# Layer 2's first product in two runs of 256 columns instead of one of 512

## The chip, the cores and the metric

The kernel runs on one core of a Trainium2 chip. The metric is the time on the device of one execution in microseconds; of several executions the median counts.

## What is computed

Attention with a local window and a few global keys over 2 batches of 8 heads, 768 positions and 64 columns per head, and behind it two feed-forward layers on 1536 rows of 512 columns:

```
def reference(**kwargs):
    attn_out = _attn_ref(**attn_kwargs)
    B, H, S, D = attn_out.shape
    x = np.ascontiguousarray(attn_out.transpose(0, 2, 1, 3)).reshape(B * S, H * D)
    x = _moe_ref(x=x, **moe_kwargs)
    return _moe2_ref(x=x, **moe2_kwargs)

def _moe_ref(x, w_in, w_out):        # w_in 512x2048, w_out 2048x512
    h = x @ w_in
    g = np.maximum(0.01 * h, h)
    return (g @ w_out).astype(np.float32)

def _moe2_ref(x, w_in, w_out, a, b):
    h = x @ w_in
    h2 = h * h
    h3 = h2 * h
    P = a[0] + a[1] * h + a[2] * h2 + a[3] * h3
    Q = 1.0 + np.abs(b[0]) * np.abs(h) + np.abs(b[1]) * h2
    g = P / (Q + 1e-06)
    return (g @ w_out).astype(np.float32)
```

The weights arrive as 64-bit floats and are decoded on the chip.

## The kernel before

Each number that goes into a large product is kept as a sum of two parts, a high one and a low one (xh and xl, gh and gl, and two halves of each weight tile), in a 4-byte format. A product of two such numbers is three matmuls: high by high, high by low, low by high.

**Attention** goes first, head pair by head pair. A score (line 377, tile sc) is a matmul of 64 partitions: the even head of a pair lies on partitions 0 to 63, the odd one on 64 to 127, and their matmuls are written alternately. The moving operand has 256 columns, or 128 for a head's first block. The values (lines 434 and 435, tile o) have 65 columns.

**The layers** are 96 units: two layers, in each 3 tiles of 512 rows of x, in each 16 blocks of 128 of the 2048 inner columns. In the code l is the layer, t the tile, f the block, and TT = 512. A unit's first product, `h_steps` (line 606, tile h), is 12 matmuls: 4 blocks c of the 512 inner rows by the three pairs of parts. The stationary operand is a 128x128 piece of the weight tile, the moving one 512 columns of xh or xl, and all 12 add into one bank of PSUM (512 numbers per partition) that `bank()` gives out in turn from two. Then the activation reads the whole bank: `act_1` in layer 1, `emit_act_2` in layer 2, on ScalarE, VectorE and GpSimd, and leaves gh and gl. The second product, `emit_y`, is again 12 matmuls of 512 columns: line 727 in layer 1, line 729 in layer 2, where a piece of gh or gl is stationary. Line 660 makes gl, in layer 2 mostly on GpSimd.

The order on each engine is that of the code. The loop in `run` writes for each unit u first h of u, then y of unit u - 2, and then the activation; so TensorE has h and y in turn. A weight tile of layer 2 comes back decoded from DRAM while layer 1 ends. Another path of the program, with attention over all keys, is skipped by a branch for these inputs; it holds a second copy of the layers that doesn't run.

Of the kernel before, what the change touches and what calls it, by code (L numbers as in the profile page):

```python
# [17 lines left out]
P = 128  # L18
# [7 lines left out]
def attention_moe_moe2(  # L26
# [15 lines left out]
    nc = tc.nc  # L42
# [7 lines left out]
    NK = DM // P  # L50
    NF = DFF // P
    TT = 512
# [62 lines left out]
    xh = xpool.tile([P, NK, NT], F32R, name="xh")  # L115
    xl = xpool.tile([P, NK, NT], F32R, name="xl")
# [465 lines left out]
    class Layers:  # L582
# [16 lines left out]
        def h_steps(self, u):  # L599
            l, t, f = self.units[u]  # L600
            wt = (self.w1, self.w2)[l][f]
            cs = slice(t * TT, (t + 1) * TT)
            h = self.state["h", u] = self.bank()
            for c in range(NK):
                for n, (m, xs) in enumerate(((0, xh), (0, xl), (1, xh))):
                    nc.tensor.matmul(  # L606
                        h,
                        wt[:, m, c * P : (c + 1) * P],
                        xs[:, c, cs],
                        start=c == 0 and n == 0,  # L610
                        stop=c == NK - 1 and n == 2,
                    )
                yield

        def new_g(self, u):
            gh, gl = (self.tpool.tile([P, TT], F32R, tag=n, name=n) for n in ("gh", "gl"))
# [448 lines left out]
```

## Time and profile before

| what | us |
|---|---|
| median of 3 runs | 642.52 |
| lowest and highest of them | 641.34, 643.16 |
| span of the profiled execution, first to last instruction | 639.8 |
| median less that span | 2.7 |
| TensorE busy | 625.5 |
| VectorE busy | 472.1 |
| ScalarE busy | 438.6 |
| GpSimd busy | 207.8 |

The profile gives for its execution only the span, not a time of its own with what lies around it; the last 2.7 us come from setting the span against the median. The recorded duration of a matmul holds its way through the array and overlaps with the next, so the rate of matmuls is read from their starts, or from blocks of the chain of waits.

### The profile page before, as it was taken

The page shows a single profiled execution, that of the slowest core. Times are in us where ns is not written, and L with a number is a line of the kernel's source. Part 1 is how long each engine was busy: PE and PEld are TensorE (multiplying, and loading weights), DVE is VectorE, ACT ScalarE, POOL GpSimd, SP SyncE. Part 2 cuts the span into 40 slices and gives each one's busy share as a digit, 9 for nine tenths or more (in the row PEclk, how much of TensorE's full clock was granted, in tenths as well). Part 3 has the DMA queues.
Part 4 walks back from the last instruction along what each step waited for, and adds up shares of the span by engine and source line. Part 5 has one row for each costly group of instructions (what it writes and reads, how often), then busy time and mean ns, then how long its engine had stood idle before and what let it go on. Part 6 is the DMA issues. An engine that isn't in the chain of part 4 may idle for free.

```text
span 639.8 us, 9604 instructions
## 1 busy us (share of the span) xinstructions
PE 625.5 (98%) x3264; PEld 526.1 (82%) x3264; DVE 472.1 (74%) x933; ACT 438.6 (69%) x830; POOL 207.8 (32%) x220
## 2 busy tenths in 40 slices
PE   6999999999999999999999999999999999999995
PEld 4999998888888888888888888888888888888884
DVE  6888988887886555555444479997777777897784
ACT  4788997777876545455334477876677888866672
POOL 2887884344443433332000002222222222112220
PEclk9999999999999999999999999999999999999999
DMA  8775861755268776765323310000023332100002
GB/s 189 171 190 139 184 155 67 252 192 191 73 202 241 216 234 209 225 220 171 95 97 98 100 33 34 1 1 0 1 92 106 96 97 72 48 19 1 2 0 73
DMA packets 81323, 73.35 MB, mean 115 GB/s; under 512 B 51248, under 2 KB 67888, under 8 KB 81264
## 3 DMA queue, kind: packets, MB, share of 16 engines
q1 hardware_dynamic: 80752, 72.11, 38.4%
q8 instruction: 28, 0.46, 0.3%
q0 software_dynamic: 80, 0.39, 0.1%
q14 instruction: 31, 0.25, 0.1%
q10 hardware_dynamic: 432, 0.13, 0.1%
HBM read 60.69 MB, written 11.93 MB: 113 GB/s over the span
## 4 chain that ended last, share of the span: by engine, by line
PE 95%; DVE 3%; DMA 1%; issue 0%; ACT 0%; SPq 0%; DVEq 0%
PE h L606 41%; PE y L729 21%; PE y L727 20%; PE pt L413 3%; PE sc L377 3%; PE o L435 2%; PE o L434 2%; PE h L306 2%; DVE sn L388 1%; PE h L199 1%; DMA qr<-in_q_dram 1%; PE o L432 0%; DVE pts L421 0%; DVE xl L205 0%; DVE w L164 0%
## 5 line engine op out<-in xcount | busy, mean ns | idle before, releaser
L606 PE MATMUL h<-xh,w 128*128 128x512 f32 x768 | 253.0, 390 | 0.0
L606 PEld LDWEIGHTS h<-xh,w 128*128 128x128 f32 x768 | 144.2, 188 | 30.0
L606 PE MATMUL h<-xl,w 128*128 128x512 f32 x384 | 149.4, 389 | 0.0
L660 POOL TENSOR_TENSOR gl<-u,gh 128x512 fp32r<-128x512 f32 x44 | 57.0, 1296 | 265.0 <-PE y L729 129.6
L727 PE MATMUL y<-gh,w 128*128 128x512 f32 x384 | 126.1, 389 | 0.0
L729 PE MATMUL y<-w,gh 128*128 128x512 f32 x384 | 125.6, 389 | 0.0
L155 POOL TENSOR_TENSOR dec<-dec,wraw 128x512 int32<-128x512 int32 x48 | 64.0, 1342 | 82.7 <-DVE wraw L142 79.0
L727 PEld LDWEIGHTS y<-gh,w 128*128 128x128 f32 x384 | 72.1, 188 | 15.0
L729 PEld LDWEIGHTS y<-w,gh 128*128 128x128 f32 x384 | 72.1, 188 | 14.9
L606 PEld LDWEIGHTS h<-xl,w 128*128 128x128 f32 x384 | 72.1, 188 | 14.5
L729 PE MATMUL y<-w,gl 128*128 128x512 f32 x192 | 75.1, 391 | 0.0
L727 PE MATMUL y<-gl,w 128*128 128x512 f32 x192 | 74.7, 389 | 0.0
L631 DVE TENSOR_TENSOR gl<-h,gh 128x512 fp32r<-128x512 f32 x48 | 33.0, 688 | 51.9 <-ACT gh L630 51.9
L630 ACT ACTIVATE gh<-h 128x512 fp32r<-128x512 f32 x48 | 28.6, 597 | 59.0 <-PE y L727 53.5
L682 ACT ACTIVATE h<-h 128x512 f32<-128x512 f32 x48 | 28.7, 597 | 52.8 <-PE h L606 52.7
L626 DVE SCALAR_TENSOR_TENSOR h<-h,g 128x512 f32<-128x512 f32 x48 | 33.3, 695 | 27.2 <-ACT g L625 27.0
L670 DVE SCALAR_TENSOR_TENSOR w<-w,epsq,h 128x512 f32<-128x512 f32 (+1 forms) x49 | 36.2, 740 | 20.9 <-ACT h L694 20.3
L625 ACT ACTIVATE g<-h 128x512 f32<-128x512 f32 x48 | 28.6, 597 | 31.1 <-PE h L606 30.9
L402 ACT ACTIVATE pr<-sn,st 128x256 f32<-128x256 f32 (+1 forms) x96 | 47.8, 500 | 1.3 <-DVE st L388 1.1
L684 DVE SCALAR_TENSOR_TENSOR w<-h,coef,w 128x512 f32<-128x512 f32 x48 | 35.9, 748 | 16.1 <-ACT w L683 16.0
L729 PEld LDWEIGHTS y<-w,gl 128*128 128x128 f32 x192 | 36.0, 188 | 8.6 <-POOL gl L660 1.1
L727 PEld LDWEIGHTS y<-gl,w 128*128 128x128 f32 x192 | 36.1, 188 | 7.4
(113 smaller groups left out, 1120.5 us busy)
## 6 DMA issues: line engine op xcount, KB each, us to landing
wraw<-in_moe_w_in_dram SPq DMA_DIRECT2D x24, 512.0 KB, 4.6
wraw<-in_moe_w_out_dram SPq DMA_DIRECT2D x24, 512.0 KB, 4.5
scratch<-dec SPq DMA_DIRECT2D x32, 256.0 KB, 5.5
wf<-scratch SPq DMA_DIRECT2D x16, 512.0 KB, 3.4
w<-in_moe_w_in_dram SPq DMA_DIRECT2D x8, 512.0 KB, 4.2
w<-in_moe_w_out_dram SPq DMA_DIRECT2D x8, 512.0 KB, 4.8
vc<-in_v_dram SPq DMA_DIRECT2D x16, 192.0 KB, 3.2
qkraw<-in_q_dram SPq DMA_DIRECT2D x6, 512.0 KB, 3.5
```

The costliest lines, as they stand in the source:

```text
L155: nc.gpsimd.tensor_tensor(ti, ti, self.c, ALU.add)
L402: nc.scalar.activation(self.pr[:, :w], self.sn[:, :w], AF.Exp, bias=self.least_at, scale=-1.0,)
L606: nc.tensor.matmul(h, wt[:, m, c * P : (c + 1) * P], xs[:, c, cs], start=c == 0 and n == 0, stop=c == NK - 1 and n == 2,)
L625: nc.scalar.activation(g, h, AF.Copy)
L626: nc.vector.scalar_tensor_tensor(h, h, 0.01, g, ALU.mult, ALU.max)
L631: nc.vector.tensor_tensor(gl, h, gh.bitcast(F32), ALU.subtract)
L660: (nc.gpsimd if on_pool else nc.vector).tensor_tensor(gl, g, gh.bitcast(F32), ALU.subtract)
L670: nc.vector.scalar_tensor_tensor(ow[:, cs], ow[:, cs], epsq, oh2[:, cs], ALU.add, ALU.mult)
L682: nc.scalar.activation(h2, h, AF.Square)
L684: nc.vector.scalar_tensor_tensor(w0, h2, coef[:, 7:8], w0, ALU.mult, ALU.add)
L727: nc.tensor.matmul(ys[d], wt[:, m, ds_], gs, start=st, stop=sp)
L729: nc.tensor.matmul(ys[d], gs[:, ds_], wt[:, m, :], start=st, stop=sp)
```

## The change

Layer 1 keeps its one run over 512 columns. In layer 2 the 12 matmuls of `h_steps` are made twice: once into the left 256 columns of the bank, from the left 256 columns of xh and xl, and once into the right ones. Each of the 24 matmuls has its own weight load, and the second run loads the same 12 weight pieces again. The bank, its readers and the second product are as before.

```
         def h_steps(self, u):
             l, t, f = self.units[u]
             wt = (self.w1, self.w2)[l][f]
-            cs = slice(t * TT, (t + 1) * TT)
             h = self.state["h", u] = self.bank()
-            for c in range(NK):
-                for n, (m, xs) in enumerate(((0, xh), (0, xl), (1, xh))):
-                    nc.tensor.matmul(
-                        h,
-                        wt[:, m, c * P : (c + 1) * P],
-                        xs[:, c, cs],
-                        start=c == 0 and n == 0,
-                        stop=c == NK - 1 and n == 2,
-                    )
-                yield
+            cols = [(0, TT)] if l == 0 else [(0, TT // 2), (TT // 2, TT)]
+            for a, b in cols:
+                for c in range(NK):
+                    for n, (m, xs) in enumerate(((0, xh), (0, xl), (1, xh))):
+                        nc.tensor.matmul(
+                            h[:, a:b],
+                            wt[:, m, c * P : (c + 1) * P],
+                            xs[:, c, t * TT + a : t * TT + b],
+                            start=c == 0 and n == 0,
+                            stop=c == NK - 1 and n == 2,
+                        )
+                    yield
```

On TensorE one unit's first product in layer 2 stands like this in the program before; the row ahead is the last matmul of a y block, a row names line, operation, what is written and read, and the size of the output, and "waits" names the semaphores (DVE is VectorE) that the instruction waits for:

```order
L729 MATMUL y_4510<-w_4002,gh 128x512
L606 MATMUL h<-xh,w_4119 128x512 [waits DVE_49]
L606 MATMUL h<-xl,w_4119 128x512
L606 MATMUL h<-xh,w_4119 128x512 x2
L606 MATMUL h<-xl,w_4119 128x512
L606 MATMUL h<-xh,w_4119 128x512 x2
L606 MATMUL h<-xl,w_4119 128x512
L606 MATMUL h<-xh,w_4119 128x512 x2
L606 MATMUL h<-xl,w_4119 128x512
L606 MATMUL h<-xh,w_4119 128x512
```

These are its 12 matmuls, with one wait, for the readers of the bank. The same unit in the changed program, where line 606 has become 607, again from the last matmul of the y block ahead:

```order
L730 MATMUL y_4546<-w_4002,gh 128x512
L607 MATMUL h<-xh,w_4119 128x256 [waits DVE_49,PE_49]
L607 MATMUL h<-xl,w_4119 128x256
L607 MATMUL h<-xh,w_4119 128x256 x2
L607 MATMUL h<-xl,w_4119 128x256
L607 MATMUL h<-xh,w_4119 128x256 x2
L607 MATMUL h<-xl,w_4119 128x256
L607 MATMUL h<-xh,w_4119 128x256 x2
L607 MATMUL h<-xl,w_4119 128x256
```

Here stand the first 11 of its 24 matmuls; the rest go on in the same pattern, and no row says where the second run begins. The first matmul has a second wait, for TensorE's own semaphore (PE): its value is that of the last matmul of the unit two before, which wrote the same bank. The first two units of layer 2 don't have it, the other 46 do. Nothing else moves on any engine.

## Rows read from the trace of the kernel before

**Rows 1.** The page: span, and the chain that ended last, by engine and line.
```profile
span 639.8 us, 9604 instructions
...
PE 95%; DVE 3%; DMA 1%; issue 0%; ACT 0%; SPq 0%; DVEq 0%
PE h L606 41%; PE y L729 21%; PE y L727 20%; PE pt L413 3%; PE sc L377 3%; PE o L435 2%; PE o L434 2%; PE h L306 2%; DVE sn L388 1%; PE h L199 1%; DMA qr<-in_q_dram 1%; PE o L432 0%; DVE pts L421 0%; DVE xl L205 0%; DVE w L164 0%
```

**Rows 2.** That chain in order of time, layer 2: start, length, engine, instructions.
```profile
365.76 2.72 PE h L606 x12
368.48 2.72 PE y L727 x12
...
384.80 2.97 PE y L729 x12
...
412.24 2.91 PE y L729 x12
...
420.59 2.72 PE h L606 x12
423.56 2.83 PE y L729 x11
426.39 2.72 PE h L606 x12
...
619.51 2.72 PE h L606 x12
622.23 10.91 PE y L729 x48
```

**Rows 3.** Busy time by engine from first to last h, granted clock, DMA.
```profile
core 0: us, PE busy (x) PEld busy (x) DVE busy (x) ACT busy (x) POOL busy (x), PEclk, DMA share, GB/s
...
365.76:622.23 256.47, 256.44 (x1129) 211.48 (x1129) 210.17 (x301) 193.17 (x325) 56.12 (x44) 1.00 0.12 38
```

**Rows 4.** Matmuls and weight loads (PEld) in order of time, layer 2: start, length.
```profile
387.60 0.39 PE L606 MATMUL h<-xh,w 128*128 128x512 f32 x1
387.83 0.39 PE L606 MATMUL h<-xl,w 128*128 128x512 f32 x1
...
387.61 0.19 PEld L606 LDWEIGHTS h<-xl,w 128*128 128x128 f32 x1
387.83 0.41 PEld L606 LDWEIGHTS h<-xh,w 128*128 128x128 f32 x2
```

**Rows 5.** Matmuls in order of time at the first wait for gl.
```profile
384.98 0.50 PE L729 MATMUL y<-w,gl 128*128 128x512 f32 x1
385.31 0.62 PE L729 MATMUL y<-w,gh 128*128 128x512 f32 x2
```

**Rows 6.** Score matmuls in order of time, two places in attention.
```profile
62.35 0.39 PE L377 MATMUL sc<-kh,qh 64*128 64x256 f32 x2
62.57 0.28 PE L377 MATMUL sc<-kl,qh 64*128 64x256 f32 x2
...
63.05 0.28 PE L377 MATMUL sc<-kh,ql 64*128 64x256 f32 x2
...
86.47 0.28 PE L377 MATMUL sc<-kl,qh 64*128 64x256 f32 x2
...
86.93 0.28 PE L377 MATMUL sc<-kh,ql 64*128 64x256 f32 x2
```

**Rows 7.** Weight loads of the values, in order of time.
```profile
60.20 0.30 PEld L434 LDWEIGHTS o<-vp,pts 128*128 128x128 f32 x2
60.42 0.30 PEld L435 LDWEIGHTS o<-vc,pts 128*128 128x128 f32 x2
```

**Rows 8.** Weight loads of scores of 128 columns, in order of time.
```profile
46.36 0.19 PEld L377 LDWEIGHTS sc<-kl,qh 64*128 64x128 f32 x2
...
46.59 0.19 PEld L377 LDWEIGHTS sc<-kh,qh 64*128 64x128 f32 x2
```

**Rows 9.** Line 606 by itself: count, ns min/median/max, first and last start.
```profile
L606 PEldq EVENT_SEMAPHORE  x7: 51/51/51, 149.9 to 183.6; - x7
its engine sat idle before it (us, times) until:
```

## The prediction

> **What bounds the kernel now.** I read the page first. The chain of waits that ended last lies 95% on TensorE, and 41% of the span is on line 606, the first products of both layers [rows 1]. Then I read that chain in order of time, where layer 2 stands as blocks of 12 matmuls: h, y, h, y, each 2.72 us [rows 2]. So a matmul of 512 columns begins every 2.72 / 12 = 0.2267 us, without a pause. The first h of layer 2 begins at 365.76 and the last ends at 622.23: 256.47 us for 94 blocks (48 of h, 46 of y), of which 94 x 2.72 = 255.7 are matmuls. The remaining 0.8 us stand at three y blocks (2.97, 2.91, and 3.08 from the end of the h before 423.56 to 426.39), where TensorE waited for gl. In this stretch the granted clock is 1.00, the 2.4 GHz level, while VectorE is busy 210 of 256 us, ScalarE 193 and GpSimd 56 [rows 3]. TensorE sets the end here. A change of x in each unit's first product is worth 48 x there, and the others only get slack.
>
> Next comes the weight load. Each matmul has its own, and the load for the next one begins as the present one begins [rows 4]. What a load costs without this cover is seen at the first of the three waits, where the load itself had waited for gl: from that matmul to the next pass 385.31 - 384.98 = 0.33 us [rows 5] in place of 0.227, so a load of 128 columns takes 0.11 us when it stands alone. Under 512 columns it has 0.227 us of cover. Under 256 it will have about half, and that is the whole question.
>
> **The change part by part.** Layer 2 has 48 units of 12 matmuls, 576 of 512 columns, in all 576 x 0.2267 = 130.6 us. They become 1152 of 256 columns, with 576 more weight loads. The data that pass through the array stay the same: 24 x 256 = 12 x 512 columns. So the sum is 1152 x P - 130.6, with P the time from one run of 256 to the next.
>
> The trace has no stream of single 128-row matmuls of 256 columns, so I bound P from both sides. Three things can set it.
>
> First the columns. At 2.4 GHz 512 columns need 213.3 ns, and the rows show 226.7. If the 13.3 ns above that belong to each instruction, 256 columns take 120.0; if they go with the columns, 113.3. The attention scores are of 256 columns. In their first step a matmul follows 62.57 - 62.35 = 0.22 us after the one ahead of it [rows 6]; that contains one uncovered load of 0.11, so 0.11 remain for 256 columns, against 0.33 - 0.11 = 0.22 for 512. Twice the columns, twice the time: that speaks for 113.3.
>
> Second the loads. The values in attention have matmuls of only 65 columns, which leave the loads as the limit: two loads begin at 60.20 and the next two at 60.42, 0.11 each [rows 7]; the scores of 128 columns have the same step, loads at 46.36 and two steps later at 46.59, 0.115 [rows 8]. So loads that follow each other allow about 112 ns. This forbids a P far below 113.3 (at 112 the sum is 129.0 - 130.6 = -1.5 us, the limit of any gain), and it stands just beside the 113.3 of the columns.
>
> Third, both together. Where scores of 256 columns run under each other's loads, four steps take 63.05 - 62.57 = 0.48 in one place and 86.93 - 86.47 = 0.46 in another [rows 6]: P = 115 to 120. This is the nearest row by its shape. But there two heads run side by side, on partitions 0 to 63 and 64 to 127, so each step holds two loads and two matmuls that share TensorE's order; the changed layer has one of each. I take 113.3 as the floor that columns give, add 0.7 for a load that ends so close to its end, and get P = 114. That lies nearer to the floor than to the scores because the step of the values, also a single stream of 128 rows, holds its 0.11 without a surplus. This is where I chose. The sum is 1152 x 0.1140 - 130.6 = +0.8 us, and both ends stay: 112 gives -1.5, 120 gives 138.2 - 130.6 = +7.7.
>
> The Trainium skill, page "TensorE: Matmul & The Clock Gate", section "Measured speedup vs the span model", puts about 4 ns of issue on each further tile that runs beside another. By it a pair's step would be 113.3 + 4 = 117.3, an estimate, and the surplus of the scores would be the pair's own. The same page, "Back-to-back issue gap", gives columns / 2.4 + 2.5 ns; by it the split would cost 576 x 2.5 ns = 1.4 us. The row of 226.7 for 512 columns disagrees with its 215.8, so I don't use it.
>
> The rest costs nothing that I can find. The order shows a second wait at the head of 46 of the 48 units, on TensorE's own semaphore. The value is that of the last matmul into the same bank, the unit two before; three blocks, 8 us, lie between [rows 2], so it is long reached. A second wait becomes an instruction of its own for the sequencer, and layer 1 has seven such at this line, 51 ns each [rows 9], and no idle time of TensorE is listed before line 606; the sequencer runs them while the matmul ahead still streams. If that cover were gone: 46 x 51 ns = 2.3 us. Behind each stands only its own h, and behind that y. Readers of h (ScalarE, then VectorE) wait for the whole bank as before, so the first half is no earlier for them; no DMA moves. The three waits for gl stay, since h grows by 0.02 us per unit.
>
> Span 639.8 and the 2.7 us that the median of the three runs (642.5) has above it: 639.8 + 0.8 + 2.7 = **643.3 us**, 0.1% above the median. About 0.3%, 1.9 us here, is what a measurement of this kernel can tell from no change; P = 115.0 is where that bound is crossed.
>
> **The rivals.**
> *The step of the scores (slower).* Load and columns are of nearly equal length, and each step pays a few ns for their meeting, whether or not a second head runs beside. P = 115 to 120, middle 117.5: 1152 x 0.1175 - 130.6 = +4.8, 647.3 us, and 650.2 at 120. For it: the scores are the only rows of 256 columns, and none of their longer series falls below 115. Against it: the pairs, and the proportion in rows 5 and 6. It decides from P = 115 on; the waits for gl could give back at most their 0.8.
>
> *Loads come out from under the matmuls (slower by much).* If a load had to wait for the matmul before it, each of the 576 added runs would cost 0.11 us more: 576 x 0.11 = +63 us, 706. Against it: loads begin with the matmul ahead in every row of layer 2 [rows 4], though with 128 rows they all use the same partitions. A small part of it, a load late now and then, is what would carry the time past 650. The same page, section "The mechanism", says that a load overlaps a running matmul only where the row group differs; by that rule this rival would hold. The trace disagrees: a step of 226.7 ns has no room for 213 of columns and 110 of load.
>
> *Faster.* Loads limit to 112 and the columns' surplus goes with a shorter run: -1.5 us, 641.0. It would still be within the bound; beyond it the three waits for gl would have to vanish as well, -0.8 more, and nothing makes gl earlier.
>
> **How the numbers follow.** Forecast 0.55 (own range 641.0 to 644.4), the step of the scores 0.37, loads uncovered in part or whole 0.05, faster 0.03. So faster 0.03, within 0.3% 0.55, slower 0.42. The range reaches from the load limit, 641.0, to P = 120, 650.2; the two cases inside it hold over 0.9, but the second is too likely to cut off.
>
> **What the profile after would show.** In the chain of waits the h blocks of layer 2 have 24 matmuls and last 2.72 to 2.76 us (P 113.3 to 115), while y stays at 2.72; from the first h to the end of the last 256.5 to 258.4 us. By the scores' step h lasts 2.76 to 2.88 and that stretch 258.4 to 264.2; with uncovered loads h lasts up to 4.0. Loads number 3264 + 576 = 3840, each beginning with the matmul ahead. Idle time on TensorE at the heads of h blocks, behind the new wait, or a lower granted clock in layer 2, would show me wrong in a way that I did not price. The prediction falls if P is above 115, and P is the one number that no row gives.

## The result, and the profile after

The changed kernel takes 650.01 us (median of 4 runs, 648.83 to 651.12); the kernel before took 641.95 us beside it (4 runs). The ratio is 1.0126, 95% interval 1.0114 to 1.0138, so the change costs 8.1 us, between 7.3 and 8.9. A second comparison (experiment 8) gave 1.0138. The time lies inside the range of the prediction, at its upper end, and not at the forecast of 643.3.

The chain of waits of the changed kernel in order of time (start, length, engine, instructions), from the end of layer 1 on and at the end; it answers to [rows 2]:

```profile
362.44 2.72 PE h L607 x12
365.16 2.72 PE y L728 x12
367.88 2.87 PE h L607 x24
370.75 2.75 PE y L728 x12
...
381.99 2.75 PE y L730 x12
...
629.28 2.87 PE h L607 x24
632.15 10.94 PE y L730 x48
```

Each h block of layer 2 has 24 matmuls and lasts 2.87 us in place of 2.72. Each y block behind one lasts 2.75, although nothing in it was changed. From the first h of layer 2 to the end of the last it is 632.15 - 367.88 = 264.27 us, against 256.47 [rows 2]: +7.8. That is 48 x 0.15 = 7.2 for h and about 46 x 0.03 = 1.4 for y, less the 0.8 of the three waits for gl, which are gone: no y block between these rows is longer than the others. (This execution's span is 649.3, 9.5 more than the one before, since its attention also ran 2.1 us longer, ahead of any changed instruction: the first h of layer 1 begins at 108.7 and not at 106.6. The change doesn't bring that: when the same kernel was profiled again in experiment 8 it began at 107.1. The medians differ by 8.1.)

The same stretch by engine, which answers to [rows 3]:

```profile
367.84:632.15 264.31, 264.31 (x1706) 241.73 (x1705) 210.51 (x301) 193.08 (x325) 56.39 (x44) 1.00 0.11 37
```

TensorE (first figure after the length) is busy without a gap at a granted clock of 1.00, the 2.4 GHz level; the others do the same work as before in more time. So the loss is in TensorE's own steps. Matmuls and weight loads at the head of one h block, which answers to [rows 4]:

```profile
502.37 0.39 PE L730 MATMUL y<-w,gh 128*128 128x512 f32 x1
502.60 0.28 PE L607 MATMUL h<-xh,w 128*128 128x256 f32 x1
502.71 0.28 PE L607 MATMUL h<-xl,w 128*128 128x256 f32 x1
502.83 0.40 PE L607 MATMUL h<-xh,w 128*128 128x256 f32 x2
...
502.60 0.19 PEld L607 LDWEIGHTS h<-xl,w 128*128 128x128 f32 x1
502.71 0.31 PEld L607 LDWEIGHTS h<-xh,w 128*128 128x128 f32 x2
```

The first step is 0.11 us, the next 0.12, and so it stays: 24 steps in 2.87 us are 0.1196 on average. Loads still begin as the matmul ahead begins, so none came out from under the matmuls. From the last y matmul to the first h matmul it is 0.23 us as ever, with the second wait in between. Line 607 by itself:

```profile
L607 PEldq EVENT_SEMAPHORE  x53: 51/51/51, 151.9 to 627.1; - x53
its engine sat idle before it (us, times) until:
who waited for it (us, times):
```

These are the 7 separate waits of layer 1 [rows 9] and the 46 new ones, 51 ns each, with no idle time behind them. And the head of a y block:

```profile
499.73 0.28 PE L607 MATMUL h<-xh,w 128*128 128x256 f32 x1
499.85 0.40 PE L730 MATMUL y<-w,gh 128*128 128x512 f32 x1
500.08 0.40 PE L730 MATMUL y<-w,gl 128*128 128x512 f32 x1
500.32 0.62 PE L730 MATMUL y<-w,gh 128*128 128x512 f32 x2
```

The steps 500.08 - 499.85 = 0.23 and 500.32 - 500.08 = 0.24 are longer than the 0.227 of an undisturbed row of 512. By the starts of the single matmuls the steps of this block are 233, 236, 228, 233, 230 and from then on 226 to 227 ns. That is the 0.03 us of each y block.

### The profile page after: what moved, and what is told of

It is laid out like the page before. It is cut to its first block, busy times and chain, and to the rows that moved or that the text cites. A ratio compares the mean times of both kernels' runs of the same rounds, so it can differ in the third digit from the quotient of the medians.

```text
span 649.3 us, 10846 instructions
## 1 busy us (share of the span) xinstructions
PE 635.7 (98%) x3840; PEld 558.5 (86%) x3840; DVE 472.5 (73%) x933; ACT 438.6 (68%) x830; POOL 207.9 (32%) x220
## 4 chain that ended last, share of the span: by engine, by line
PE 95%; DVE 3%; DMA 1%; issue 0%; ACT 0%; SPq 0%; DVEq 0%
PE h L607 41%; PE y L730 20%; PE y L728 20%; PE pt L413 3%; PE sc L377 3%; PE o L435 2%; PE o L434 2%; PE h L306 2%; DVE sn L388 1%; PE h L199 1%; DMA qr<-in_q_dram 1%; PE o L432 0%; DVE pts L421 0%; DVE xl L205 0%; DVE w L164 0%
## 5 line engine op out<-in xcount | busy, mean ns | idle before, releaser
L607 PE MATMUL h<-xh,w 128*128 128x256 f32 (+1 forms) x1152 | 272.5, 319 | 0.0
L607 PEld LDWEIGHTS h<-xh,w 128*128 128x128 f32 x1152 | 194.9, 190 | 16.5
L607 PE MATMUL h<-xl,w 128*128 128x256 f32 (+1 forms) x576 | 183.4, 318 | 0.0
L607 PEld LDWEIGHTS h<-xl,w 128*128 128x128 f32 x576 | 109.6, 190 | 9.1
L388 DVE CUSTOM_DVE_ANT_0 sn<-sc,bias 128x256 f32<-128x256 f32 (+1 forms) x96 | 34.0, 395 | 11.9 <-PE sc L377 11.7
```

What stands on the lines that cost most here:

```text
L388: nc.vector.tensor_tensor_reduce(self.sn[:, :w], self.sc[:, :w], bias[:, 2 * self.pair.hp + self.j, b0 : b0 + w], -0.125, 3.0e38, ALU.add, ...
L607: nc.tensor.matmul(h[:, a:b], wt[:, m, c * P : (c + 1) * P], xs[:, c, t * TT + a : t * TT + b], start=c == 0 and n == 0, stop=c == NK - 1 ...
```

## The experiments

What was in dispute: why a step of 256 columns takes 120 ns, when its columns need 113 in proportion and its load 112. Three theories went in: a fixed 13.3 ns for each matmul; columns in proportion with a load that takes 120; and a load that is slowed by the columns streaming beside it.

**1, a probe of single steps.** The kernel before, with 24 extra matmuls of a chosen kind ahead of each first product in layer 2; N columns, M weight columns, K partitions:

```
+            if l == 1:
+                N, M, K, same = PROBES[u % 16]
+                for r in range(24):
+                    c = 0 if same else r % NK
+                    nc.tensor.matmul(
+                        h[0:M, 0:N],
+                        wt[0:K, 0, c * P : c * P + M],
+                        xh[0:K, c, t * TT : t * TT + N],
+                        start=r == 0,
+                        stop=r == 23,
+                    )
             for c in range(NK):
```

> The kernel before, with 24 extra matmuls ahead of each unit's first product in layer 2, into the same bank, whose results the first product then overwrites. The kind of the extra matmuls changes with the unit's f: columns 512, 448, 384, 320, 288, 256, 224, 192, 128, 64 at 128x128 weights, then 256 columns with weights of 96, 64 and 32 columns, 256 with the same weights each time, 256 with 64 partitions, 128 with 64 weight columns. The step from matmul to matmul is read for each. Theory 1, a fixed 13.3 ns on top of columns at 2.4 GHz: 200.0 for 448, 173.3 for 384, 146.7 for 320, 133.3 for 288, 120 for 256, and still 120 with 64 weight columns. Theory 2, columns in proportion (0.4427 ns each) and a weight load that takes 120 from start to start: 198.3, 170.0, 141.7, 127.5, then 120 for everything of 256 columns and below with 128 weight columns, and 113.3 for 256 columns with 64 weight columns. Theory 3, as 2, but the load is only slowed while columns stream: 120 at 256, falling towards 112 at 64 columns.

It took 795.2 us. Matmuls of the probe in order of time, a row for each kind (some of the kinds; the shapes are partitions*weight columns and output):

```profile
365.87 5.60 PE L615 MATMUL h<-xh,w 128*128 128x512 f32 x24
376.75 5.03 PE L615 MATMUL h<-xh,w 128*128 128x448 f32 x24
...
414.37 3.04 PE L615 MATMUL h<-xh,w 128*128 128x256 f32 x24
422.71 2.83 PE L615 MATMUL h<-xh,w 128*128 128x224 f32 x24
...
447.17 2.76 PE L615 MATMUL h<-xh,w 128*128 128x64 f32 x24
...
463.58 2.89 PE L615 MATMUL h<-xh,w 128*64 128x256 f32 x24
471.77 2.99 PE L615 MATMUL h<-xh,w 128*32 128x256 f32 x24
...
488.50 3.12 PE L615 MATMUL h<-xh,w 64*128 64x256 f32 x24
```

A row's length holds 23 steps and the duration of one matmul. With 0.39 for 512 columns the step is (5.60 - 0.39) / 23 = 0.2265; with 0.28 for 256 it is (3.04 - 0.28) / 23 = 0.120. By the starts of the single matmuls (mean of the steps after the first) the steps are 226.6 ns for 512 columns, 202.9 for 448, 174.6 for 384, 146.6 for 320, 131.6 for 288, 119.95 for 256, and 111.6 to 111.8 for 224, 192, 128 and 64. With 256 columns they are 113.5 at 64 weight columns and 117.8 at 32. The first step of a row with 128 weight columns, which this mean leaves out, is shorter: 199 ns for 448 columns, 143 for 320, 113 for 256.

So the fixed 13.3 ns fall: 64 weight columns bring 256 columns down to 113.5, and 448 take 202.9 and not 200. The first steps speak against them too, since at 0.443 ns per column (226.6 / 512) they would be 198.3, 141.7 and 113.3, with nothing added. A load of 120 falls too: the floor of the loads is 111.7, for 224 columns as for 64. The third theory wanted the step to fall slowly below 256, and it is on the floor at 224. None of the three holds as it stood. What the rows with 128 weight columns show: from the second step on, the step is the larger of 0.443 ns per column and 111.7 ns, plus a surplus. The surplus is 6.6 ns at 256 columns, about 4 to 5 at 288 to 448, and nothing at 512.

The last row speaks of the pairs in the scores: 64 partitions, one head alone, has 119.3 ns per step by its starts, which is within the 115 to 120 of the pairs in [rows 6]. The same weights each time changed nothing (119.95).

**2 and 3, other places to split.** Only the columns differ from the changed kernel:

```
-            cols = [(0, TT)] if l == 0 else [(0, TT // 2), (TT // 2, TT)]
+            cols = [(0, TT)] if l == 0 else [(0, 384), (384, TT)]
```

> Layer 2's first product in runs of 384 and 128 columns instead of two of 256. Theory 1 (fixed 13.3 ns): 173.3 + 120 = 293.3 ns a pair instead of 226.7, 576 x 66.7 = +38.4 us over the kernel before. Theory 2 (proportion, load 120): 170 + 120 = 290, +36.5 us. Theory 3: 170 + about 114, +33 us. If the cost were only one of a second instruction per pair (13.3 ns as measured for 256 + 256), it would stay at +7.7.

Measured: 677.11 us against 642.20, ratio 1.0541 (1.0518 to 1.0564), +34.9 us. With 320 in place of 384:

> Layer 2's first product in runs of 320 and 192 columns. Theory 1: 146.7 + 120 = 266.7 ns a pair, 576 x 40 = +23.0 us over the kernel before. Theory 2: 141.7 + 120 = 261.7, +20.2 us. Theory 3: 141.7 + about 117, +18.4 us.

Measured: 660.47 us, ratio 1.0284 (1.0263 to 1.0305), +18.3 us. The chains of waits have, for the split at 384,

```profile
429.24 3.39 PE h L607 x24
432.63 2.80 PE y L730 x12
```

and for the split at 320

```profile
426.00 3.07 PE h L607 x24
429.08 2.77 PE y L730 x12
```

With 48 blocks of h, 46 of y and the 0.8 of the waits for gl given back that makes 48 x 0.67 + 46 x 0.08 - 0.8 = +35.0 and 48 x 0.35 + 46 x 0.05 - 0.8 = +18.3: the measured loss. For the split at 384 it lies between the second theory's 36.5 and the third's 33, for that at 320 it meets the third's 18.4; one price for a second instruction, +7.7, is far off. From the probe's steps alone, 174.6 + 111.7 and 146.6 + 111.8 ns a pair, the h blocks should cost 576 x 59.6 = +34.3 and 576 x 31.7 = +18.3; part of what h saves against that comes back in y, whose first step by the starts is 285 ns behind the split at 384 and 251 behind that at 320, in place of 227. The short run of a pair never pays less than the floor of the loads, so the further from the middle, the dearer.

**4, both layers**, twice the dose: every h split in two runs of 256.

```
-            cols = [(0, TT)] if l == 0 else [(0, TT // 2), (TT // 2, TT)]
+            cols = [(0, TT // 2), (TT // 2, TT)]
```

> The change made in both layers, so twice the dose: 96 units split instead of 48. If the price is that of the runs of 256 themselves (7.3 us on the h blocks and 1.2 on the y blocks behind them), it doubles to about +16.5 us over the kernel before, ratio 1.026. If it belongs to layer 2 (the second wait, gl as the stationary operand), it stays near +8.

Measured: 658.98 us, ratio 1.0271 (1.0249 to 1.0293), +16.8 us. The price is that of the runs. Its chain of waits shows the same two lengths in layer 1, and line 607 has only 56 separate waits, 53 in the changed kernel:

```profile
150.14 2.87 PE h L607 x24
153.01 2.75 PE y L728 x12
...
L607 PEldq EVENT_SEMAPHORE  x56: 51/51/51, 115.4 to 634.1; - x56
```

Ten of the 56 lie in layer 1, before 187 us, and its 48 units still cost as much as those of layer 2. So neither the separate second wait nor gl as the stationary operand, which layer 1 doesn't have, makes the price.

**5, a second probe**, with other kinds in the table of the first.

> The same kind of probe as the first, 24 extra matmuls ahead of each unit's first product in layer 2, overwritten by it; other kinds: 240, 248, 264, 272, 480 and 496 columns with 128 weight columns; 256 columns with 112, 80, 48 and 16 weight columns; 512, 448, 384 and 320 with 64, and 512 and 448 with 32 weight columns. The first probe left open what the surplus of a step is, over the larger of 0.4427 ns per column and the 111.7 ns floor of the loads. Theory A, load and stream slow each other for as long as the load lasts: the surplus falls with the weight columns (256 columns: about 119 with 112, 115 with 80, 113.3 with 48 and 16; none at 320 to 512 with 64 or 32) and grows smoothly from 240 (about 113 to 116) to 272 (about 127). Theory B, the surplus is a matter of phase, of where in some fixed beat a matmul begins, and not of the length of the load: with few weight columns it is as irregular as with 128 (117.8 at 32 weight columns was seen, 113.5 at 64), and neighbouring column counts jump (240 at 111.7, 264 and 272 off a straight line by several ns).

It took 825.9 us. Rows as above:

```profile
365.33 2.84 PE L615 MATMUL h<-xh,w 128*128 128x240 f32 x24
373.49 2.92 PE L615 MATMUL h<-xh,w 128*128 128x248 f32 x24
381.69 3.04 PE L615 MATMUL h<-xh,w 128*128 128x264 f32 x24
...
423.24 2.96 PE L615 MATMUL h<-xh,w 128*16 128x256 f32 x24
...
442.48 5.72 PE L615 MATMUL h<-xh,w 128*32 128x512 f32 x24
...
492.81 5.44 PE L615 MATMUL h<-xh,w 128*128 128x496 f32 x24
```

By the starts 240 columns take 111.8 ns, 248 115.1, 264 120.0, and 272 125.7. So 264 columns take the same time as 256 (3.04 in both rows). With fewer weight columns 256 need 113.7 at 80, 117.2 at 48 and still 116.7 at 16, while 512 columns with 32 weight columns need 231.7, more than with 128; 496 need 220.0 (the last row). Theory A, by which the surplus goes with the length of the load, falls. Theory B, that it is irregular and a matter of lengths fitting each other, holds as far as that goes; it doesn't say what the lengths must fit.

**6, 7 and 8, splits chosen by the probes**, with the changed kernel run again beside them. The edit is that of experiment 2, with 264 and with 240.

> Layer 2's first product in runs of 264 and 248 columns. If the steps of the probes hold in the kernel (120.0 and 115.1 ns), a pair takes 235.1 ns and the split costs 576 x 8.4 = +4.8 us over the kernel before on the h blocks, about +5 with the other terms: clearly less than two runs of 256 (239.9, +7.6 on the h blocks). If a second run has one fixed price (13.3 ns a pair, as 256 + 256 measured), the split costs the same +8 as 256 + 256.

> Layer 2's first product in runs of 240 and 272 columns. By the steps of the probes 111.8 + 125.7 = 237.5 ns a pair, 576 x 10.8 = +6.2 us on the h blocks, about +6.5 in all, between the split at 264 and that at 256. With one fixed price for a second run: +8. With columns in proportion and the 111.7 ns floor of the loads alone, and no surplus: 111.7 + 120.4 = 232.1, +3.1.

> The changed kernel again, for comparison with the splits at 264 and 240 on the same chip: +8 us, ratio 1.0126 as before. Should the split at 264 be as slow as this one, the probes' steps don't carry over into the kernel.

Measured, against 642.49 us: split at 264 646.18 us, ratio 1.0057 (1.0044 to 1.0070), +3.7; split at 240 647.14 us, 1.0074 (1.0061 to 1.0088), +4.7; the changed kernel again 651.02 us, 1.0138 (1.0123 to 1.0153), +8.5. So both cost less than two runs of 256, as the probes' steps had it, and a fixed price of a second run falls: 8 columns more in one run and fewer in the other give back over half of the loss. That the split at 264 is cheaper than that at 240, as the same steps had it, isn't shown, since the two intervals overlap. Both came out below their expected figures, about +5 and +6.5. The chains of waits, first of the split at 264:

```profile
421.32 2.82 PE h L607 x24
424.14 2.72 PE y L730 x12
```

and of the split at 240:

```profile
422.22 2.83 PE h L607 x24
425.04 2.72 PE y L730 x12
```

Here h takes 0.10 and 0.11 us more than before, 48 x 0.10 = 4.8 and 48 x 0.11 = 5.3. The y blocks are back at 2.72 to 2.73, so that term of the loss goes away, and the waits for gl give back up to 0.8: some 4.0 and 4.5 us, inside both intervals. By the starts the 272 columns of the split at 240 take about 124 ns in the kernel and not the probe's 125.7. None of these versions is faster than the kernel before.

**9, where the operands lie.** The probe again, all at 128x128 weights, with the place of the moving columns, of the result and the distance between columns changed (three operands of its matmul, without the lines around them):

```
+                        h[:, at : at + N],
+                        wt[:, 0, w0 + c * P : w0 + (c + 1) * P],
+                        x[:, c, x0 : x0 + N * stride : stride],
```

> A probe as before (24 extra matmuls ahead of each unit's first product in layer 2, overwritten by it), all with 128x128 weights; what changes is where the operands lie: 256 columns from moving column 0, 4, 8, 16, 64 and 256, into bank column 0, 64 and 256, with every second column, and from xl in place of xh; 384 columns from moving column 0, 64 and 128 and into bank column 128; 128 columns with every second one; 496 from column 16. Theory B1, the surplus comes from where in a fixed beat a matmul begins, so from lengths alone: 120.0 for all of 256 columns and 174.6 for all of 384, wherever they lie. Theory B2, it comes from load and stream meeting in the same piece of memory: it changes with the moving column (from 113.3 to 120 for 256, from 170 to 178 for 384) and not with the bank column.

It took 812.9 us. Rows in order of time: 256 columns from moving column 0, 8 and 64, then 256 with every second column, and at the end 128 with every second and 496 from column 16:

```profile
367.67 3.04 PE L618 MATMUL h<-xh,w 128*128 128x256 f32 x24
...
384.31 2.96 PE L618 MATMUL h<-xh,w 128*128 128x256 f32 x24
...
400.88 3.04 PE L618 MATMUL h<-xh,w 128*128 128x256 f32 x24
...
434.24 5.68 PE L618 MATMUL h<-xh,w 128*128 128x256 f32 x24
...
492.22 2.96 PE L618 MATMUL h<-xh,w 128*128 128x128 f32 x24
500.47 5.60 PE L618 MATMUL h<-xh,w 128*128 128x496 f32 x24
```

By the starts the step of 256 columns is 119.95 from column 0, 64 and 256, but 118.6, 116.6 and 117.9 from column 4, 8 and 16. The bank column makes no difference (119.95 at 0, 64 and 256), nor does xl in place of xh (120.0) or 384 columns' place (174.6 in all four). So neither pure theory stands: not lengths alone, since 8 columns' shift gives 3 ns back; not a meeting in memory that would reach from 113.3 to 120. What is plain is the columns' own rate. 256 columns of which every second is taken need 229.8 ns, as much as 512 in a row, and 128 such need 116.6, about as much as 256 in a row. At this distance the time goes with the stretch of memory that is read and not with the columns that pass; other distances weren't tried.

## Why the prediction was right in its range and wrong in its forecast

**What bounds the kernel: right.** TensorE, without a gap, at clock 1.00; 48 units, 1152 runs. The sum 1152 x P - 130.6 has the right shape: with P = 2.87 / 24 = 0.1196 it gives +7.2, and the h blocks measured 48 x 0.15 = 7.2.

**The range: in part luck.** It was built on 642.5 for the kernel before and ended at +7.7, P = 120. The loss is 8.1, 0.4 more, and 650.01 lies inside only because the kernel before took 641.95 beside it; experiment 8's 651.02 lies outside. Most of the rest over the h blocks' 7.2 is a term that the sum didn't have, the y blocks (below).

**P: wrong.** The step that failed is "I take 113.3 as the floor that columns give, add 0.7". P is 119.6 on average, so the rival "the step of the scores" came true, near its upper end; it had 0.37 where the forecast had 0.55. The floor itself was read rightly: the first step of each block is 113 ns, and experiment 1 gives the loads 111.7. What was wrong is the 0.7 for the two together, and the reason to set aside [rows 6]. I put the surplus of the scores down to two heads running side by side. Experiment 1 ran 64 partitions, one head alone, and got 119.3, so the surplus belongs to a single stream too. The Trainium skill (page "TensorE: Matmul & The Clock Gate", section "Measured speedup vs the span model") has about 4 ns for a further tile, which I took as support. The estimate of 117.3 from it agrees with the pairs' 115 to 120 only by size, since the single stream needs no second tile for its 119.3. The nearest row by shape was the right one, and I talked it away by a cause that no row showed.

**The row of the values**, which I used against a surplus, told of the loads alone. With 65 columns nothing but the load sets the step. It can't tell what happens when the two lengths are near each other.

**What I priced at nothing:** the second wait cost nothing, as said: 46 new wait instructions, no idle time, 0.23 us from y to h. The y blocks behind it are the term I missed: +0.03 us each, 1.2 to 1.4 us in all, because a row of 512 columns that is entered from a row of 256 takes five steps to get back to 0.227 (233, 236, 228, 233, 230 ns). The waits for gl, which were to stay, went away and gave back their 0.8, as the rival's text said they could at most.

**The other rivals.** Loads stay under the matmuls: all 3840 are there, each 2 to 5 ns behind the start of the matmul ahead where I looked, and a step of 119.6 ns has no room for 113 of columns and 110 of load. The Trainium skill (page "TensorE: Matmul & The Clock Gate", section "The mechanism") has a line by which a load overlaps a running matmul only in another row group. These runs disagree: load and matmul both use all 128 rows, and in a step of 119.6 ns they overlap. Nothing made it faster; splits at 264 and 240 are slower than one run, too, and the granted clock in layer 2 stayed at 1.00.

**Open.** What the surplus is. With 128 weight columns it is 6.6 ns at 256 columns, 0 at 512, 3.1 at 264 and 0.1 at 240, and a row from column 0 has none in its first step. It doesn't follow the length of the load (experiment 5) or the bank (9), and it depends a little on where the moving columns begin (9). Load and stream read the same memory at the same time, but that this is the cause is only argued; no run takes the two apart.

## What to carry to other kernels

Halve the columns of a matmul and the work in the array stays the same, but its weight load loses half of its cover. Read the load's own step from start to start (here 111.7 ns for 128 weight columns) and the columns' (here 0.443 ns each), and where the shorter run comes near the load, expect a surplus over both: put a row of such matmuls into the kernel and read the step. When the nearest row by shape speaks against a floor that was built from other rows, believe the row, unless a row shows the cause by which it would not apply.

## What was unexpected of the hardware

- 264 columns take the same 120.0 ns per step as 256, and 496 columns take 220.0 from column 0 but 226.7, the time of 512, from column 16.
- Every second column of 512 costs about as much (229.8 ns) as all of them (226.6), so gaps of one column in the moving operand are paid for.
- Fewer weight columns don't always help: 256 columns take 113.5 ns with 64 weight columns, 117.8 with 32 and 116.7 with 16.
